# Token sum of phi(k) by eight accumulating DMAs instead of 32 matmuls, in a linear-attention and MLP-mixer kernel

## Chip, cores, metric

One core of one Trainium2 chip. The metric is the device time of one execution in microseconds (us), lower is better. The kernel before takes 267.94 us (median of 6 runs, 267.54 to 268.09, so 0.2% apart).

## The reference, cut to what matters

```python
B, S, D = 1, 2048, 640;  H = 32; Dh = 20
q, k, v = ...                                   # from x @ wqkv
phi = lambda t: jnp.where(t > 0, t + 1, jnp.exp(t)) + 1e-6
pq, pk = phi(q), phi(k)
kv  = jnp.einsum("bhsd,bhse->bhde", pk, v)
z   = jnp.einsum("bhsd->bhd", pk)               # the token sum: 640 numbers
den = jnp.einsum("bhqd,bhd->bhq", pq, z)[..., None] + 1e-6
o   = num / den                                 # then @ wo; this is branch a
# branch b: LayerNorm, W1, gelu, token shifts, W2, LayerNorm, W3, gelu, W4
return g * a + (1 - g) * b
```

The case is about `z`: the sum over 2048 tokens of `phi(k)`, and when the denominators that need it can be computed.

## The kernel before

TensorE (PE) runs as one long stream: the K stage (16 chunks of 128 tokens), the Q stage (10 units, with the x-times-phi(k) products "G" woven in), the W1 stage, W2, then W3 and W4. `pk` holds phi(k) as bf16, 128 partitions by 16 chunks by 640. The token sum is 32 narrow matmuls against ones, each onto 32 of the 128 output partitions, in turn onto the four groups of 32 (all 32 took 1.20 us in the trace), in the middle of the Q stage; two units later, ten one-column matmuls turn it into per-partition columns.

```python
def z_rows():                                   # after Q unit 2, counted from 0
    p = alloc()
    for (n0, n1) in COLS:                       # 512 + 128 columns
        for cc in range(0, NCH, 4):
            for q in range(4):
                mm(PP[p][32*q:32*(q+1), n0:n1], lhsT=ones32[:], rhs=pk[:, cc+q, n0:n1],
                   start=(cc == 0), stop=(cc == NCH-4), tile_position=(0, 32*q), ...)
    act(zsb[:], PP[p][:, 0:D], ACT.Copy)
    release(p)
    nc.vector.tensor_copy(zhi[:], zsb[:])       # high and low bf16 parts
    nc.vector.tensor_tensor(zlo[:], zsb[:], zhi[:], op=ALU.subtract)

def z_cols():                                   # after Q unit 4
    p = alloc()
    ...
    for j in range(DC):
        mm(PP[p][:, j:j+1], lhsT=zh[:, j], rhs=c32[:], start=True, stop=False)
        mm(PP[p][:, j:j+1], lhsT=zl[:, j], rhs=c32[:], start=False, stop=True)
    nc.vector.tensor_copy(zT[:], PP[p][:, 0:DC])
    release(p)
    for j in range(DC):                         # Zb: masks times column, for the denominators
        nc.vector.tensor_scalar(Zb[:, j, :], mask32, zT[:, j:j+1], None, op0=ALU.mult)
```

Two other users of POOL (GpSimd) matter, by their place in its program: in the trace, POOL stood 27.03 us at the copies that come first here, and the LayerNorm scales behind them started after them, at 33.24 us:

```python
# in late_loads(), before the K stage: waits for the load of W1
for g in range(4):
    nc.gpsimd.tensor_copy(w1x4[:, :, g, :], w1g[:, :, g, P:CG])

def ln1_sq(c):                                  # LayerNorm scale of four chunks at a time
    act(junk[:], x_sb[:, c, :], ACT.Square, accum_out=sq[:, c:c+1])
    if c % 4 == 3:
        ...                                     # five small POOL instructions -> rs1
def ln1_apply(c):                               # VectorE (DVE) needs rs1, then SP transposes by DMA
    nc.vector.tensor_scalar(lx[:], x_sb[:, c, :], me[:, c:c+1], rs1[:, c:c+1], ...)
    sp.dma_start_transpose(lnxT[:, :, c*P:(c+1)*P], lx[:])
```

And the start of the W1 stage:

```python
w1_unit(0, 4); den_unit(); rec_piece(0); w1_unit(0, 0); kv_unit(); rec_piece(1); w1_unit(0, 1)
m_unit(0); m_unit(1); ...
```

## Time and profile before

| | before |
|---|---|
| median time | 267.94 us |
| span of the profiled execution | 266.3 us |
| PE busy | 259.6 us (97%) |
| the 32 matmuls of the token sum, in the chain of waits | 1.20 us |

From the page of the kernel before: busy us per engine, then three rows over 40 equal slices of the span (6.66 us each) with the busy share of PE, the granted PE clock and the mean share of the 16 DMA engines, in tenths.

```profile
PE 259.6 (97%) x1666; PEld 136.1 (51%) x1699; DVE 116.0 (44%) x212; ACT 110.7 (42%) x165; POOL 32.9 (12%) x111
...
PE   7999999999999999999999999999999999999995
...
PEclk9999999999999999999999999999999999999999
DMA  6999993431340269932652001001000000001001
```

PE is never idle for long (97% busy) and never slow (mean granted clock 0.999), so the time is the length of its stream. The DMA row: from the second to the sixth slice (7 to 40 us) the DMA engines are full (9 in the row; a share of 1.04 to 1.32 in the windows from 13 to 40 us), because first x and then the weights for the later stages load then.

From the chain of work that ended last, in order of time (start, us, what): the token sum sits in it.

```profile
43.06 1.20 PE pp L364 x32
```

From the POOL timeline (start, us, instruction; in brackets the idle time before it and what ended it):

```profile
31.98 1.27 POOL L304 COPY w1x<-RB 128x160 bf16<-128x160 bf16 x4 [27.03 <-DMA RB<-in_B_w_dram]
33.24 0.23 POOL L218 TENSOR_SCALAR me<-ym 128x4 f32<-128x4 f32 x1
```

POOL stands for 27 us at the four copies that wait for the W1 load. Whatever is put behind them in POOL's program starts at about 33.3 us in this trace, and not before.

From the PE timeline, the first W1 unit, the denominators, and the second W1 unit:

```profile
73.59 2.32 PE L423 MATMUL pp<-lnxT,w1x 128*128 128x512 bf16 x10
75.84 1.26 PE L470 MATMUL pp<-pqT,Zb 128*32 128x512 bf16 x20
77.04 2.33 PE L423 MATMUL pp<-lnxT,RB 128*128 128x512 bf16 x9
```

A W1 unit costs PE about 2.2 us from start to next start.

### The profile page before, as it was taken

What the parts mean: (1) busy time and instruction counts of PE and PEld (TensorE: products, weight loads), DVE (VectorE), ACT (ScalarE), POOL (GpSimd) and SP (SyncE); (2) the same over time, 40 slices, a digit from 0 to 9 for tenths busy, and PEclk for the clock granted to TensorE, in tenths of its full rate; (3) what the DMA queues carried; (4) which work ended last, traced back from release to release, by engine and by line L of the source; (5) the groups of instructions that cost most, each with busy time, mean ns of one, the idle gap of its engine ahead of it and who ended that gap; (6) DMA issues with size and microseconds to landing.
All of it is one profiled execution on the core that took longest, in us unless ns stands there. A gap on an engine that the chain in (4) does not pass through costs nothing.

```text
span 266.3 us, 4195 instructions
## 1 busy us (share of the span) xinstructions
PE 259.6 (97%) x1666; PEld 136.1 (51%) x1699; DVE 116.0 (44%) x212; ACT 110.7 (42%) x165; POOL 32.9 (12%) x111
## 2 busy tenths in 40 slices
PE   7999999999999999999999999999999999999995
PEld 3555555555545445554444455555544444555552
DVE  2486748665655065999930033233200002233232
ACT  3466663665355771244977522022034444022020
POOL 5000132020200000536870000000000000000000
PEclk9999999999999999999999999999999999999999
DMA  6999993431340269932652001001000000001001
GB/s 204 169 192 301 365 225 68 62 75 25 77 98 0 59 213 362 313 83 49 101 100 49 0 2 49 27 25 49 27 25 0 2 0 0 25 27 49 27 25 49
DMA packets 42245, 23.95 MB, mean 90 GB/s; under 512 B 31090, under 2 KB 41458, under 8 KB 42226
## 3 DMA queue, kind: packets, MB, share of 16 engines
q1 hardware_dynamic: 41474, 22.99, 36.1%
q10 hardware_dynamic: 720, 0.69, 0.8%
q8 instruction: 13, 0.21, 0.3%
q14 instruction: 6, 0.05, 0.1%
q0 software_dynamic: 32, 0.00, 0.0%
HBM read 12.86 MB, written 3.44 MB: 61 GB/s over the span
## 4 chain that ended last, share of the span: by engine, by line
PE 95%; DMA 2%; issue 1%; DVE 0%; SPq 0%
PE pp L638 20%; PE pp L571 19%; PE pp L423 8%; PE pp L597 8%; PE pp L390 8%; PE pp L556 8%; PE pp L261 8%; PE pp L252 8%; DMA RXH<-in_A_x_dram 2%; PE pp L580 2%; PE pp L623 1%; PE pp L632 1%; PE pp L587 1%; PE pp L457 1%; PE pp L443 1%
## 5 line engine op out<-in xcount | busy, mean ns | idle before, releaser
L638 PE MATMUL pp<-RB,RXH 128*128 128x128 bf16 (+1 forms) x381 | 53.5, 297 | 0.7 <-issue 0.3
L571 PE MATMUL pp<-lnxT,RA 128*128 128x512 bf16 x235 | 51.9, 379 | 0.3
L638 PEld LDWEIGHTS <-RXH 128*128 128x128 bf16 x390 | 29.7, 98 | 24.2 <-issue 2.1
L571 PEld LDWEIGHTS <-RA 128*128 128x128 bf16 x240 | 23.4, 98 | 28.0
L600 ACT ACTIVATE RXH<-pp,g_all 128x640 f32<-128x640 f32 x16 | 12.7, 794 | 54.9 <-PE pp L597 54.9
L573 ACT ACTIVATE RXH<-pp 128x1024 bf16<-128x1024 f32 x24 | 24.2, 1019 | 26.7 <-PE pp L571 26.7
L244 ACT ACTIVATE eb<-pp 128x640 bf16<-128x640 f32 (+1 forms) x26 | 21.4, 828 | 25.2 <-PE pp L390 16.3
L261 PE MATMUL pp<-RPK,RXH 128*128 128x128 bf16 (+1 forms) x157 | 25.0, 297 | 0.2
L252 PE MATMUL pp<-RA,RXT 128*128 128x512 bf16 (+1 forms) x157 | 24.0, 300 | 0.2
L390 PE MATMUL pp<-RXT,RA 128*128 128x512 bf16 x97 | 23.1, 379 | 0.2
L597 PE MATMUL pp<-Mp,pqT 128*128 128x512 bf16 (+1 forms) x158 | 23.0, 298 | 0.1
L602 DVE SCALAR_TENSOR_TENSOR RPK<-RPK,omg,RXH 128x640 f32<-128x640 f32 x8 | 7.1, 885 | 36.5 <-ACT RXH L600 36.5
L556 PE MATMUL pp<-w,RXH 128*128 128x128 bf16 (+1 forms) x157 | 21.7, 297 | 0.2
L423 PE MATMUL pp<-lnxT,RB 128*128 128x512 bf16 x77 | 18.1, 379 | 0.2
L261 PEld LDWEIGHTS <-RXH 128*128 128x128 bf16 x160 | 12.7, 98 | 10.4
L247 DVE TENSOR_SCALAR eb<-eb 128x640 bf16<-128x640 bf16 (+1 forms) x26 | 9.5, 365 | 19.3 <-ACT eb L244 19.3
L602 DVE SCALAR_TENSOR_TENSOR RXT<-RXT,omg,RXH 128x640 f32<-128x640 f32 x8 | 7.1, 884 | 24.6 <-ACT RXH L600 24.6
L252 PEld LDWEIGHTS <-RXT 128*128 128x128 bf16 x160 | 12.6, 98 | 9.5 <-DVE RA L329 0.2
L597 PEld LDWEIGHTS <-pqT 128*128 128x128 bf16 x160 | 12.2, 98 | 10.0 <-issue 0.8
L556 PEld LDWEIGHTS <-RXH 128*128 128x128 bf16 x160 | 12.3, 98 | 9.6
L607 DVE SCALAR_TENSOR_TENSOR RXH<-pp,omg,RXT 128x640 bf16<-128x640 f32 x8 | 7.1, 884 | 19.8 <-PE pp L638 19.8
L390 PEld LDWEIGHTS <-RA 128*128 128x128 bf16 x100 | 11.1, 118 | 8.9
(110 smaller groups left out, 238.4 us busy)
## 6 DMA issues: line engine op xcount, KB each, us to landing
out_dram<-RXH SPq DMA_DIRECT2D x15, 160.0 KB, 1.8
RA<-in_B_w_dram SPq DMA_DIRECT2D x5, 432.0 KB, 6.9
RA<-in_A_wqkv_dram SPq DMA_DIRECT2D x2, 800.0 KB, 8.9
RB<-in_B_w_dram SPq DMA_DIRECT2D x1, 1120.0 KB
RXH<-in_A_x_dram SPq DMA_DIRECT2D x2, 480.0 KB, 4.7
RB<-in_B_w_dram SPq DMA_DIRECT2D x1, 960.0 KB, 13.6
RB<-in_B_w_dram SPq DMA_DIRECT2D x1, 800.0 KB, 8.5
Mp<-Mscr SPq DMA_DIRECT2D x1, 800.0 KB
```

The costliest lines, as they stand in the source:

```text
L244: act(e[:, 0:n], src, ACT.Exp)
L252: mm(PP[p][:, n0:n1], lhsT=xT[:, dc, c * P:(c + 1) * P], rhs=wkg[:, dc, n0:n1], start=(dc == 0), stop=(dc == DC - 1))
L261: mm(PP[p][:, n0:n1], lhsT=x_sb[:, c, i * P:(i + 1) * P], rhs=pk[:, c, n0:n1], start=(c == 0), stop=(c == NCH - 1))
L390: mm(PP[p][:, tt * 512:(tt + 1) * 512], lhsT=wqp[:, dc, j], rhs=xT[:, dc, t0:t0 + 512], start=(dc == 0), stop=(dc == DC - 1))
L423: mm(PP[p][:, tt * 512:(tt + 1) * 512], lhsT=lh, rhs=lnxT[:, dc, t0:t0 + 512], start=(dc == 0), stop=(dc == DC - 1))
L556: mm(PP[p][:, n0:n1], lhsT=hsT[:, fc, 2 + c * P:2 + (c + 1) * P], rhs=w2[:, fc, n0:n1], start=(fc == 0), stop=(fc == DC - 1))
L571: mm(PP[p][:, k * 512:(k + 1) * 512], lhsT=w3[:, dc, (fc + k) * P:(fc + k + 1) * P], rhs=lnxT[:, dc, t * 512:(t + 1) * 512], start=(dc == ...
L573: act(h2T[:, t % 2, fc:fc + 2, :], PP[p][:].rearrange("p (k s) -> p k s", k=2), ACT.Gelu_apprx_tanh)
L597: mm(PP[p][:, n0:n1], lhsT=pqT[:, j, c * P:(c + 1) * P], rhs=Mp[:, j, n0:n1], start=(j == 0), stop=(j == DC - 1))
L600: act(ga, PP[p][:, 0:D], ACT.Copy, scale=g_all[:, c:c + 1])
L602: nc.vector.scalar_tensor_tensor(x1(c), x1(c), omg[:, c:c + 1], ga, op0=ALU.mult, op1=ALU.add)
L638: mm(PP[p][:, n0:n1], lhsT=h2T[:, k, fc, cc], rhs=w4[:, fc, n0:n1], start=False, stop=(fc == NF - 1))
```

## The change

The intent: take the 1.2 us of matmuls off PE. The sum over chunks becomes eight DMAs of two chunks each (bf16 source, float32 destination, with `accum_op` add from the second on), issued by POOL between the middle of the K stage and the end of the Q stage. Below, each of these DMAs is a link of the chain, and the moment when its data have arrived is its landing. Each waits for the one before, as they update the same bytes. A DVE addition joins the two halves, and the column matmuls move from the Q stage behind the first W1 unit.

```diff
-    Mp = sb("Mp", DC * D)[:].rearrange("p (j d) -> p j d", j=DC)
+    RMP = sb("RMP", DC * D)
+    Mp = RMP[:].rearrange("p (j d) -> p j d", j=DC)
+    zacc = RMP[:, 0:4 * D].bitcast(F32)
 (ones32 and c32 become onec, one column of ones)
+    def z_add(k):
+        nc.gpsimd.dma_start(zacc, RPK[:, 2 * k * D:2 * (k + 1) * D],
+                            **({"accum_op": ALU.add} if k else {}))
+    def z_sum():
+        nc.vector.tensor_tensor(zsb[:], zacc[:, 0:D], zacc[:, D:2 * D], op=ALU.add)
+        nc.vector.tensor_copy(zhi[:], zsb[:])
+        nc.vector.tensor_tensor(zlo[:], zsb[:], zhi[:], op=ALU.subtract)
 (K stage, after chunk c)
+        if c in (9, 12, 15):
+            z_add(c // 3 - 3)
 (Q stage, after unit n_; z_rows is gone)
-            if n_ == 2:
-                z_rows()
-            if n_ == 4:
-                z_cols()
+            if n_ in (1, 3, 4, 6, 7):
+                z_add({1: 3, 3: 4, 4: 5, 6: 6, 7: 7}[n_])
 (end of the Q stage)
+    z_sum()
 (W1 stage)
     w1_unit(0, 4)
+    z_cols()
+    w1_unit(0, 0)
     den_unit()
     rec_piece(0)
-    w1_unit(0, 0)
     kv_unit()
```

More of the change, by code (lines that the diff above doesn't have):

```diff
@@ L103 @@
     ident = sb("ident", P)
-    ones32 = sb("ones32", 32)
-    c32 = sb("c32", 1)
+    onec = sb("onec", 1)
     mask4 = sb("mask4", P)
@@ L181 @@
         nc.gpsimd.memset(wkg[:, dc, D + 1:D + 2], 1.0)
-    nc.gpsimd.memset(ones32[:], 1.0)
-    nc.gpsimd.memset(c32[:], 1.0 / 32)
+    nc.gpsimd.memset(onec[:], 1.0)
     nc.gpsimd.memset(nhalf[:], -0.5)
@@ L342, with z_cols @@
         k_post(c, c)
+    def z_add(k):
[5 more added lines that the diff above has]
+        nc.vector.tensor_tensor(zlo[:], zsb[:], zhi[:], op=ALU.subtract)
+    def z_cols():
+        p = alloc()
+        zh = zhi[:].rearrange("p (q j) -> p j q", j=DC)
+        zl = zlo[:].rearrange("p (q j) -> p j q", j=DC)
+        for j in range(DC):
+            mm(PP[p][:, j:j + 1], lhsT=zh[:, j], rhs=onec[:], start=True, stop=False)
+            mm(PP[p][:, j:j + 1], lhsT=zl[:, j], rhs=onec[:], start=False, stop=True)
+        nc.vector.tensor_copy(zT[:], PP[p][:, 0:DC])
+        release(p)
+        for j in range(DC):
+            nc.vector.tensor_scalar(Zb[:, j, :], mask32, zT[:, j:j + 1], None, op0=ALU.mult)
     for c in range(3, NCH):
@@ L353 @@
             pop(ln1_s)
+        if c in (9, 12, 15):
+            z_add(c // 3 - 3)
     gq = [(0, c) for c in range(NCH - 3, NCH)] + [(i, c) for i in range(1, DC) for c in range(NCH)]
     wqp = wq.rearrange("p k (q j) -> p k j q", j=DC)
-    def z_rows():
-        p = alloc()
-        for (n0, n1) in COLS:
-            for cc in range(0, NCH, 4):
-                for q in range(4):
-                    mm(PP[p][32 * q:32 * (q + 1), n0:n1], lhsT=ones32[:], rhs=pk[:, cc + q, n0:n1],
-                       start=(cc == 0), stop=(cc == NCH - 4), tile_position=(0, 32 * q), skip_group_check=True)
-        act(zsb[:], PP[p][:, 0:D], ACT.Copy)
-        release(p)
-        nc.vector.tensor_copy(zhi[:], zsb[:])
-        nc.vector.tensor_tensor(zlo[:], zsb[:], zhi[:], op=ALU.subtract)
-    def z_cols():
-        p = alloc()
-        zh = zhi[:].rearrange("p (q j) -> p j q", j=DC)
-        zl = zlo[:].rearrange("p (q j) -> p j q", j=DC)
-        for j in range(DC):
-            mm(PP[p][:, j:j + 1], lhsT=zh[:, j], rhs=c32[:], start=True, stop=False)
-            mm(PP[p][:, j:j + 1], lhsT=zl[:, j], rhs=c32[:], start=False, stop=True)
-        nc.vector.tensor_copy(zT[:], PP[p][:, 0:DC])
-        release(p)
-        for j in range(DC):
-            nc.vector.tensor_scalar(Zb[:, j, :], mask32, zT[:, j:j + 1], None, op0=ALU.mult)
     n_ = 0
```

## The prediction

> **What bounds it now.** The page gives PE 259.6 of 266.3 us busy (97%) at full granted clock, and the chain of waits is 95% PE. Time is the PE stream's length plus its stalls; other engines matter only where PE waits for them.
>
> **Removed.** The groups by line show the column sum as 32 matmuls; in the chain they hold PE from 43.06 for 1.20 us, with a 0.3 us issue gap just before. So about 1.25 us (0.5%) leaves the critical path. The ACT copy of the sum (0.70 us) goes too; nothing critical waited for it. That is the whole possible gain: faster by over 2% is practically excluded.
>
> **Moved.** The ten one-column matmuls (PE about 0.65 us, 51.3 to 51.9) and their DVE copy and five masks (0.95 us) move from mid Q stage to just behind the first W1 unit. There they follow a new DVE sum (about 0.82), cast (0.49) and subtract (0.82): 2.2 us that PE now waits for directly.
>
> **Added.** Eight DMAs issued by POOL, each 128 rows of 1280 bf16 in, f32 out (655 KB written); seven also read the old 655 KB. Each waits for the one before: a serial chain. It is meant to start mid K stage (about 21 us), but in POOL's program order the first stands behind the w1x copies, which waited 27 us for the W1 load and ran from 31.98 to 33.25 (POOL timeline). So the chain starts at about 33.3, not 21.
>
> Duration of one link d: the only POOL-issued DMA in the trace, 1.2 KB, took 3.5 us to land, beside loads. [...] I take 5.4. The first competes with weight loads that land until about 42 (DMA share about 1.0 from 30 to 40): 6.3. No accumulating DMA is in the trace, so d is the weak number.
>
> Landing of the eighth (estimate): 33.3 + 6.3 + 7 x 5.4 = 77.4. DVE sum, cast, subtract: 79.6. PE, 1.25 + 0.65 us earlier than before, reaches the column matmuls at about 74.0. PE stall about 5.6 us, once, in the middle of the W1 stage; nothing later gives it back, since PE has no other slack. Had the chain been free, PE would still stand about 0.5 us at the denominators, because the masks queue on DVE behind the 1.7 us of shift copies.
>
> Sum: 267.9 - 1.25 + 5.6 = about **272.3 us** (+1.6%). Every 0.1 us of d is 0.7 us of the result; break-even near d = 4.8.
>
> Range, 8 in 10: 266.8 to 281. Chances: faster over 2% 0.01, within 2% 0.54, slower over 2% 0.45.
>
> **What would show it.** First new DMA issue at about 33.3 after the w1x copies; eight issues 5 to 6 us apart, the last landing at 74 to 81; the DVE sum of the two halves idle before it, released by that DMA; a PE idle of some us before the zhi weight loads at about 74; the K and Q stages unchanged except minus 1.9 us; every stage after shifted by one constant. LayerNorm scales of chunks 4 to 7 (POOL) come some us later, behind the third DMA; three free PSUM buffers should keep PE fed.
>
> **What would make it wrong.** d at or below 4.6: no stall, 266.7 to 267.5. [...] POOL, blocked in order, delaying LayerNorm scales enough that DVE holds up PSUM and PE stalls in the Q stage already. Transposes of the normalised rows slowed by the new traffic.

Where a cut is marked, the figures from which the author came to 5.4 us for a link, and one of the risks, have been taken out. The 5.4 us of a link and the 6.3 us of the first stand as guesses. The sum, with all its terms: 33.3 + 6.3 + 7 x 5.4 = 77.4 us for the eighth landing, from that a stall of 5.6 us, and 267.9 - 1.25 + 5.6 = 272.3 us.

## The result, and the profile after

The changed kernel takes 279.75 us (median of 6 runs, 278.53 to 281.56). Executions over 1.5% slower than the fastest of the same kernel are left out of the means. Ratios are computed as the mean time of one kernel's fast runs over that of the other's of the same rounds, so they are not quite the ratios of the medians; here 1.045, 95% interval 1.0406 to 1.0495. It is slower by 4.5%, where 1.6% was forecast.

The same lines of the page (a slice is now 7.0 us):

```profile
PE 261.1 (93%) x1635; PEld 135.8 (49%) x1667; DVE 116.3 (42%) x213; ACT 110.0 (39%) x164; POOL 40.2 (14%) x118
...
PE   8999999969905999999999999999999999999995
...
PEclk9999999999985999999999999999999999999999
DMA  6799999695896006995245200010010000001001
```

PE has a dent in the ninth slice, a hole in the twelfth, and in the thirteenth its clock is down as well. The rest is as before.

The POOL timeline after, reduced to the copies, the eight DMA issues, and one of the LayerNorm scale instructions (the last group ends likewise behind the eighth DMA):

```profile
34.05 1.11 POOL L304 COPY w1x<-RB 128x160 bf16<-128x160 bf16 x4 [29.14 <-DMA RB<-in_B_w_dram]
35.10 0.66 POOL L345 DMA_DIRECT2D RMP<-RPK  x1
...
46.05 0.96 POOL L345 DMA_DIRECT2D RMP<-RPK  x1 [8.03 <-DMA RMP<-RPK]
51.61 0.87 POOL L345 DMA_DIRECT2D RMP<-RPK  x1 [4.59 <-DMA RMP<-RPK]
...
53.67 1.05 POOL L222 TENSOR_TENSOR rs<-ve,nhalf 128x4 f32<-128x4 f32 x1
57.16 1.21 POOL L345 DMA_DIRECT2D RMP<-RPK  x1 [2.44 <-DMA RMP<-RPK]
63.65 0.87 POOL L345 DMA_DIRECT2D RMP<-RPK  x1 [5.29 <-DVE eb L247]
68.58 0.85 POOL L345 DMA_DIRECT2D RMP<-RPK  x1 [4.07 <-DMA RMP<-RPK]
...
73.51 1.11 POOL L345 DMA_DIRECT2D RMP<-RPK  x1 [1.83 <-DMA RMP<-RPK]
79.94 0.87 POOL L345 DMA_DIRECT2D RMP<-RPK  x1 [5.33 <-DMA RMP<-RPK]
```

The first link of the chain takes 10.95 us from issue to the next issue; the other six gaps are 5.56, 5.55, 6.49, 4.93, 4.93 and 6.43 us. (For one of the issues, at 63.65 us, the profile names a DVE instruction and not the landing as what ended POOL's wait; whether DVE's work delays an issue was not tested.) The time to landing of the eight, from the same DMAs' summary:

```profile
DMA to landing us min/median/max: 4.4/5.0/10.4
```

On DVE, the consequences (waits in brackets):

```profile
54.76 0.80 DVE L226 TENSOR_SCALAR lnxs<-RXH,me,rs 128x640 bf16<-128x640 bf16 x2 [6.99 <-POOL rs L222]
...
83.09 1.51 DVE L226 TENSOR_SCALAR lnxs<-RXH,me,rs 128x640 bf16<-128x640 bf16 x4 [6.54 <-POOL rs L222]
84.52 0.82 DVE L349 TENSOR_TENSOR zsb<-RMP 128x640 f32<-128x640 f32 x1
```

LayerNorm scales on POOL stand behind DMAs that wait; DVE waits for the scales, in order, and with it everything behind.

And on PE:

```profile
57.28 0.43 PE L261 MATMUL pp<-RPK,RXH 128*128 128x512 bf16 x2 [0.72 <-DVE pqT L248]
59.66 2.32 PE L390 MATMUL pp<-RXT,RA 128*128 128x512 bf16 x9 [1.95 <-DVE pqT L248]
...
74.55 2.32 PE L423 MATMUL pp<-lnxT,w1x 128*128 128x512 bf16 x10
85.92 0.20 PE L358 MATMUL pp<-onec,zhi 128*128 128x1 bf16 x1 [9.04 <-DVE zhi L350]
86.78 0.20 PE L359 MATMUL pp<-onec,zlo 128*128 128x1 bf16 x1 [0.66 <-DVE zlo L351]
...
87.97 3.62 PE L423 MATMUL pp<-lnxT,RB 128*128 128x512 bf16 x8 [0.22 <-issue]
91.52 1.27 PE L470 MATMUL pp<-pqT,Zb 128*32 128x512 bf16 x20
```

The W1 unit after the long wait runs from 87.16 to 91.52 us, 4.36 us in place of 2.17. The windows view of the same stretch shows why (window, its length, then busy us with instruction counts for PE, PEld, DVE, ACT and POOL; the last three columns are the granted clock, the DMA share and GB/s):

```profile
78.00:80.00 2.00, 0.00 (x0) 0.00 (x0) 0.00 (x0) 0.00 (x0) 0.06 (x1) 1.00 1.01 136
80.00:82.00 2.00, 0.00 (x0) 0.00 (x0) 0.00 (x0) 0.00 (x0) 1.68 (x5) 0.83 0.56 117
...
84.00:86.00 2.00, 0.08 (x1) 0.09 (x1) 1.93 (x5) 0.00 (x0) 0.00 (x0) 0.50 0.41 82
...
88.00:90.00 2.00, 2.00 (x5) 0.73 (x5) 1.85 (x9) 0.00 (x0) 0.00 (x0) 0.50 1.00 97
...
92.00:94.00 2.00, 2.00 (x39) 1.46 (x32) 1.12 (x2) 0.71 (x1) 0.00 (x0) 1.00 0.00 0
```

Some 4.5 us after PE went idle (76.9 us) its clock was halved (a mean of 0.83 from 80 to 82 us puts the step at 81.3), and it stayed halved until about 91.6. The two gaps in the Q stage (0.72 and 1.95 us, with two wide matmuls between them) left the clock full (1.00 in every window from 54 to 68 us).

The account of the 13.6 us between the two profiled spans: minus 1.25 us (matmuls and the gap ahead of them), plus 2.67 us (two gaps in the Q stage), plus 9.70 us (waits for zhi and zlo), plus 2.19 us (slow W1 unit) is 13.3 us.

### The profile page after: what moved, and what is told of

It reads as the page before. It is cut to its first block, busy times and chain, and to the rows that moved or that the text cites. A ratio compares the mean times of both kernels' runs of the same rounds, so it can differ in the third digit from the quotient of the medians.

```text
span 279.9 us, 4156 instructions
## 1 busy us (share of the span) xinstructions
PE 261.1 (93%) x1635; PEld 135.8 (49%) x1667; DVE 116.3 (42%) x213; ACT 110.0 (39%) x164; POOL 40.2 (14%) x118
## 4 chain that ended last, share of the span: by engine, by line
PE 69%; DMA 14%; SPq 7%; DVE 4%; POOL 2%; issue 2%; ACT 1%; POOLq 0%; DVEq 0%
PE pp L639 19%; PE pp L572 18%; DMA RMP<-RPK 11%; PE pp L598 8%; PE pp L557 8%; PE pp L423 8%; SPq L158 6%; DMA RB<-in_B_w_dram 3%; PE pp L581 2%; DVE lnxs L226 1%; PE pp L624 1%; SPq L155 1%; PE pp L633 1%; PE pp L308 1%; DVE pqT L248 1%
## 5 line engine op out<-in xcount | busy, mean ns | idle before, releaser
L639 PE MATMUL pp<-RB,RXH 128*128 128x512 bf16 (+1 forms) x382 | 53.9, 298 | 0.4
L574 ACT ACTIVATE RXH<-pp 128x1024 bf16<-128x1024 f32 x24 | 24.3, 1020 | 26.7 <-PE pp L572 26.7
L598 PE MATMUL pp<-RMP,pqT 128*128 128x128 bf16 (+1 forms) x156 | 22.8, 297 | 0.2
L423 PE MATMUL pp<-lnxT,RB 128*128 128x512 bf16 x78 | 19.9, 408 | 0.4 <-issue 0.4
L428 ACT ACTIVATE RXH<-pp 128x1024 bf16<-128x1024 f32 x8 | 8.2, 1027 | 22.0 <-PE pp L423 22.0
L390 PEld LDWEIGHTS <-RA 128*128 128x128 bf16 x100 | 11.2, 117 | 11.1 <-issue 2.0
```

What stands on the lines that cost most here:

```text
L390: mm(PP[p][:, tt * 512:(tt + 1) * 512], lhsT=wqp[:, dc, j], rhs=xT[:, dc, t0:t0 + 512], start=(dc == 0), stop=(dc == DC - 1))
L423: mm(PP[p][:, tt * 512:(tt + 1) * 512], lhsT=lh, rhs=lnxT[:, dc, t0:t0 + 512], start=(dc == 0), stop=(dc == DC - 1))
L574: act(h2T[:, t % 2, fc:fc + 2, :], PP[p][:].rearrange("p (k s) -> p k s", k=2), ACT.Gelu_apprx_tanh)
L598: mm(PP[p][:, n0:n1], lhsT=pqT[:, j, c * P:(c + 1) * P], rhs=Mp[:, j, n0:n1], start=(j == 0), stop=(j == DC - 1))
L639: mm(PP[p][:, n0:n1], lhsT=h2T[:, k, fc, cc], rhs=w4[:, fc, n0:n1], start=False, stop=(fc == NF - 1))
```

## The experiments

In all of them "before" ran on the same chip.

### e1: only the first DMA

```diff
-        if c in (9, 12, 15):
-            z_add(c // 3 - 3)
+        if c == 9:
+            z_add(0)
 (no z_add in the Q stage)
```

> Only the first of the eight DMAs is issued (wrong result on purpose: the token sum then holds four of sixteen chunks at most); the DVE sum, the cast, the column matmuls and the masks stay where the change put them. Theory A (the serial chain of eight DMAs is what costs): PE waits at the zhi weight loads fall from 9.7 us to under 0.7 us, both Q-stage PE gaps (2.7 us) are gone, time 266.7 to 267.6 us, so 1.2 us of removed matmuls minus about half a microsecond at the denominators. Rival B (the new place of sum, columns and masks costs by itself): 269 us or more. Neither expects the slow W1 unit after the gap (4.4 us against 2.2) to stay, if it comes from idle.

Measured: 267.1 us, ratio 0.9974 (0.9957 to 0.9992). Both Q-stage gaps and the wait for zhi are gone and the clock stays full; PE waits 0.79 us for the masks. The one DMA still took 10.7 us to land. So the new place of the sum and columns gives back some 0.4 of the 1.25 us (0.85 us lie between the medians), and all of the loss comes with the other seven links.

### e2: the LayerNorm scales ahead of the DMAs that block them

```diff
+        if c == 9: z_add(0)                    # K stage
+            for k in {1: (1, 2, 3), 5: (4, 5), 9: (6, 7)}.get(n_, ()):   # Q stage
+                z_add(k)
```

> Same eight DMAs, but POOL's LayerNorm scale groups stand before the DMAs that blocked them (one DMA, groups 0 and 1, three DMAs, group 2, two DMAs, group 3, two DMAs). Theory A (the landing of the eighth DMA sets the time, 84.4 us in the profile): the two Q-stage PE gaps (0.7 and 1.95 us) vanish, but PE then waits about 2.7 us longer for zhi, and the time stays at 279 to 280.5 us. Rival C (POOL blocked in order, which holds up DVE and so PE, is a cost of its own that adds): 277 us or less, the gap before zhi stays at 9 to 10 us.

Measured: 279.8 us, ratio 1.0448 (1.0416 to 1.048): no change. PE and then DVE of this kernel, at the columns:

```profile
84.29 0.20 PE L358 MATMUL pp<-onec,zhi 128*128 128x1 bf16 x1 [10.27 <-DVE zhi L350]
85.15 0.20 PE L359 MATMUL pp<-onec,zlo 128*128 128x1 bf16 x1 [0.66 <-DVE zlo L351]
```

```profile
82.88 0.83 DVE L349 TENSOR_TENSOR zsb<-RMP 128x640 f32<-128x640 f32 x1 [9.64 <-DMA RMP<-RPK]
```

The gaps in the Q stage have gone, PE arrives earlier, and waits longer for the same landing. The gaps in front of a fixed deadline cost nothing here. Rival C falls: POOL's blocking is visible in the trace of the changed kernel, and worth nothing by itself. Here the DVE sum is released by the eighth DMA directly, so this kernel is the base for most of what follows. Its chain runs from 33.64 to about 82.9 us.

### e3: the w1x copies out of the way

The four copies move on POOL from before the first DMA to behind the sixth.

> The w1x copies, which wait for the W1 load, move on POOL from before the first DMA to behind the sixth. Theory A with the copies as the gate: the first DMA issues at about 13 us, the second at about 24 us behind the first scale group; with links of 8 to 10 us while weights load and 5.5 us after, the eighth lands at 66 to 76 us and the time falls to 267 to 270 us. Rival D (the loads own the DMA engines until 42 us, whatever the issue time, so nothing is gained by issuing earlier): the eighth lands after 82 us, time 278 us or more.

Measured: 277.77 us, ratio 1.0376 (1.035 to 1.0402). The expectation missed. POOL and then PE of this kernel:

```profile
12.96 0.61 POOL L341 DMA_DIRECT2D RMP<-RPK  x1 [8.03 <-DVE eb L247]
...
31.11 1.05 POOL L222 TENSOR_TENSOR rs<-ve,nhalf 128x4 f32<-128x4 f32 x1
32.12 0.97 POOL L341 DMA_DIRECT2D RMP<-RPK  x1
43.14 0.87 POOL L341 DMA_DIRECT2D RMP<-RPK  x1 [10.05 <-DMA RMP<-RPK]
```

```profile
22.46 2.13 PE L252 MATMUL pp<-RA,RXT 128*128 128x512 bf16 x10 [3.68 <-DMA RXT<-in_A_x_dram]
```

The first DMA did issue at 13 us, but the second stands behind the first scale group, which waits for ACT, and issued at 32.1. What is more, in this run PE stood 3.68 us in the K stage for a load of x that had not arrived, and the second and third links took 11.0 and 10.5 us. The gate was real, but behind it is the same full set of DMA engines (9 in the page's DMA row from 14 to 62 us). The eighth landed at about 81.4 us (the DVE sum that it releases starts at 81.38), and most of the time stayed lost.

### e4: four W1 units ahead of the columns

```diff
     w1_unit(0, 4)
+    for fc in range(4):
+        w1_unit(0, fc)
     z_cols()
+    w1_unit(1, 4)
     den_unit()
 (key-value and M units between the second half's W1 units; scaling of the queries at the end)
```

> The chain is untouched; PE gets four more W1 units (8.9 us of useful work) before the column matmuls, and the later W1 units are woven with the key-value and M units instead. Theory A: the wait for zhi shrinks from 9.7 us to under 2 us, the slow clock after it goes, time 267 to 270 us (the 2.7 us in the Q stage stay: nearer 269.5). Rival E (the DMA traffic slows PE or the other engines throughout): still above 274 us.

Measured: 276.74, 277.03 and 279.68 us (a fourth run was slow), ratio 1.0373. The wait for zhi shrank as expected (the trace has 0.55 us, for zlo), but the time did not. PE of this kernel:

```profile
86.29 0.58 PE L423 MATMUL pp<-lnxT,w1x 128*128 128x512 bf16 x1 [2.55 <-DMA lnxT<-lnxs]
...
129.53 27.75 PE L567 MATMUL pp<-lnxT,RA 128*128 128x512 bf16 x118 [3.18 <-DMA lnxT<-lnxs]
```

Two new stalls, each followed by half clock (0.50 from 86 to 88 us; 0.66 on average from 130 to 135). The first: the second half's rows hang on the last LayerNorm scales, which here still stand behind the eighth DMA. The second comes from my order: five scalings of the queries (3.1 us of DVE) stand ahead of the W2 additions, and the loads of w3 and w4, issued later, meet the transposes of the second LayerNorm; e4 does not separate the two. So it says nothing for rival E; e5 repeats it without these faults.

### e5: everything that does not need the sum goes first

On top of e2: W1 units, key-value and M units before the columns, the DVE sum behind the key-value masks, the reciprocals after them, the scaling of the queries in the W3 stage.

```diff
     w1_unit(0, 4); w1_unit(0, 0); kv_unit(); w1_unit(0, 1); m_unit(0); m_unit(1)
     w1_unit(0, 2); m_unit(2); m_unit(3); w1_unit(0, 3); m_unit(4); m_unit(5)
+    z_sum(); m_move(); (loads of w3)
+    w1_unit(1, 4); z_cols(); w1_unit(1, 0); den_unit(); four rec_piece
     w1_unit(1, 1); w1_unit(1, 2); rexp_unit(); w1_unit(1, 3)
```

> Scale groups as in e2, chain untouched; everything that does not need the token sum (four W1 units, key-value and M units, 13.7 us of PE work after the first W1 unit) now stands before the column matmuls, the DVE sum behind the key-value masks, the denominators' reciprocals and the scaling of the queries later, where DVE was idle in the profile before. Theory A (chain's end near 83 us is the only thing that costs): no PE wait above 0.7 us for zhi or masks, no half clock, 266.4 to 267.4 us, faster than before by 0.2 to 0.6 per cent. Rival E (the links' traffic costs by itself[...]): 269 us or more.

Measured: 267.24 us against 267.78, ratio 0.9985 (0.9948 to 1.0023): the 12 us are back, but no gain is shown. The same chain still ended at 82.9 us, as DVE shows:

```profile
82.88 0.82 DVE L349 TENSOR_TENSOR zsb<-RMP 128x640 f32<-128x640 f32 x1 [4.16 <-DMA RMP<-RPK]
```

PE no longer asked before it. Rival E falls. PE waits 0.86 us for the masks. The kernel before was not run in this order, so what the order is worth by itself is not separated, here and in e11 and e12.

### e6: half of each row, and e7: no addition

Both on top of e2, each wrong. e6 moves 640 of 1280 elements per DMA (and doubles one half: its output still passed the comparison, so that passing proves little about this sum). e7 drops `accum_op`.

> As e2, but each DMA moves half of its row (640 of 1280 elements, wrong result on purpose). If bytes decide a link, the links behind the first fall from 5.6 us to about 3 us and the eighth lands by 65 us; if a fixed part decides, to 4 to 4.5 us[...], the eighth lands near 70 to 73 us and the time is 267 to 268.5 us.

> As e2, but the eight DMAs overwrite and do not add (wrong result on purpose): same issue, same waits, same bytes written, no read of the destination. If the read of the old sum costs, links behind the first fall by 0.8 to 1.5 us to 4.1 to 4.8 us and the eighth lands at 73 to 78 us, time 268 to 274 us; if it is free, the links stay at 5.4 to 5.7 us and the time at 279 to 280 us.

Measured: e6 274.73 us, e7 275.54 us. Both were gated late by my own order: the seventh DMA stands behind the last scale group, which waited for ACT until 67.8 and 68.2 us, and was issued at 69.3 and 69.8 us. So the times do not compare (both missed what was expected, with two runs each), but the landings do (min / median / max): e2 4.4 / 5.2 / 9.7, e6 3.3 / 3.8 / 9.0, e7 3.2 / 3.4 / 9.6 us. Adding to the old sum costs 1.8 us of a median link (5.2 against 3.4). Half the bytes save 1.4 us, so about 2.4 us of the 5.2 do not scale with bytes (3.8 minus 1.4; an estimate from these two medians). And the largest, the first link, is 9.0 us even with half the bytes, against 9.7 in e2: its length hardly depends on its own bytes.

### e8: PE kept busy while it waits

On top of e2, 42 dummy matmuls of 128x512 on the zero tile between the first W1 unit and the columns.

> As e2 with 42 dummy matmuls of 128x512 (about 9 us at full clock) on the zero tile between the first W1 unit and the column matmuls, so PE waits for the same landing but is not idle. If the half clock after the gap is caused by the idle PE, it disappears and the time falls by 2.0 to 2.6 us against e2, to 277.2 to 278 us; if the clock drop has another cause, the time stays at 279.8 us.

Measured: 277.44, 277.92 and 278.13 us (a fourth run was slow), against 279.0 to 280.6 of e2. The granted clock is 1.0 throughout, and the W1 unit after the wait takes 2.29 us, from its start to that of the denominators at 87.40:

```profile
85.11 2.32 PE L423 MATMUL pp<-lnxT,RB 128*128 128x512 bf16 x10
```

So the slow clock is the idle PE's, and costs about 2 us on top of the wait. (Between the two profiled runs lie 2.25 us, of which 0.42 are an earlier landing, 82.46 us in e8; e2 and e8 ran on different chips.)

### e9: the weight loads later

On top of e2, the loads of wv, wo and w2 are issued at the fifth Q unit (from 55.8 us in the trace).

> As e2, but the loads of the value, output and second MLP weights (wv, wo, w2, 2.4 MB), which shared the DMA engines with the first link until about 42 us, are issued about 10 us after that, at the fifth Q unit (about 50 us). If the first link's 10 us is contention with these loads, it falls to 4.5 to 6 us, and the links that then meet the loads (issued after 50 us) grow by some us in their place; the eighth lands at 78 to 83 us and the time stays within 275 to 280 us. If the first link is long for a reason of its own (first use of the queue), it stays at about 10 us.

Measured: 284.62 us, ratio 1.0636 (1.0615 to 1.0657), slower than expected. The windows view at the first link, which was issued at 33.37 us (last two columns: DMA share and GB/s):

```profile
34.00:35.00 1.00, 1.00 (x11) 0.53 (x8) 0.12 (x1) 1.00 (x2) 0.72 (x4) 1.00 0.61 225
35.00:36.00 1.00, 1.00 (x8) 0.59 (x7) 0.90 (x2) 1.00 (x3) 0.92 (x2) 1.00 1.18 425
36.00:37.00 1.00, 1.00 (x7) 0.51 (x6) 0.64 (x1) 0.16 (x1) 0.92 (x3) 1.00 0.08 13
```

Alone on the DMA engines (share 0.00 from 32 to 34 us and from 37 to 41), the first link was done after about 3.2 us (the smallest landing of this kernel), not 10. The second waited for its scale group until 41.0, so the gain was not used; and the fifth, which met the moved loads, took 12.0 us to the next issue (59.53 to 71.52). The cost goes with the loads: the link that met them was done about when they were (the large load of w2, issued at 58.70 us, took 11.8 us to land).

### e10: two accumulators, two chains of four

The second accumulator lies where the K weights were; the DMAs alternate.

```diff
+    zaccs = [RMP[:, 0:4 * D].bitcast(F32), RA[:, 0:4 * D].bitcast(F32)]
+        nc.gpsimd.dma_start(zaccs[k % 2], RPK[...], **({"accum_op": ALU.add} if k > 1 else {}))
+        for h in range(2):                      # in z_sum
+            nc.vector.tensor_tensor(zsb[:], zsb[:], zaccs[1][:, h*D:(h+1)*D], op=ALU.add)
```

> As e2, but two accumulators and so two chains of four links, interleaved on POOL: the same DMAs and bytes (one accumulating DMA fewer), a wait for every second DMA only, two more DVE additions (1.6 us). If the waiting for completions[...] is what the chain pays, three pairs of about 8 us after the first pair (13 to 15 us) end at 71 to 74 us, PE waits 2 to 5 us for zhi, 271 to 274 us. If the DMA engines' throughput limits, the end stays near 83 us and the time at 280 us or more.

Measured: 270.68 us (268.94 to 271.98), ratio 1.0103 (1.0063 to 1.0142), slightly better than expected. The same bytes written, but the last two were issued at 59.7 and 63.2 us in the trace, with median landings of 7.1 and 7.9 us in the two chains, so the end is at about 71 us (estimate from these) in place of 82.9. So a second chain takes some 12 of the single chain's 49 us away (up to 1.8 of them, by e7, because one link fewer adds to an old sum). e10 also issues its DMAs at earlier places in POOL's program, but in e2 POOL had always been idle for 2.3 us or more before it issued a link behind the first, so its places did not hold that chain up. PE still waits 1.95 and 0.66 us for zhi and zlo; DVE began the sum at 73.4 us, held by its last LayerNorm rows, which waited for transposes. And these short waits were followed by a lower clock too (7 in the page's PEclk row for the slice from 74.3 to 81.0 us); the W1 unit behind the columns took 3.94 us, to 81.67, in place of 2.17. At half clock for the first 3.5 us and full clock after, it would take as long (an estimate from these two times):

```profile
77.73 4.00 PE L425 MATMUL pp<-lnxT,RB 128*128 128x512 bf16 x10
```

The four runs fall apart by their clock: 271.73 and 271.98 us at 0.992 and 0.994, 268.94 and 269.63 us at 1.0 and 0.998.

### e11: e5 with the masks earlier

The columns move one W1 unit forward, so that the masks stand on DVE ahead of the second shift copies.

> As e5, with the column matmuls one W1 unit earlier, so that the masks stand on DVE before the second half's shift copies, and the denominators one unit earlier. The 0.9 us PE wait for the masks seen in e5 disappears; time 266.2 to 267 us, 0.3 us below e5 and 0.4 to 0.6 per cent below before, if nothing else waits.

Measured: 267.32 us (266.18 to 269.58), ratio 0.9997 (0.9962 to 1.0032). The wait for the masks is gone, as expected; now PE waits 0.47 us for zlo in the profiled run, since the chain ended at about 84.4 us this time. No gain is shown, where 0.4 to 0.6 per cent were expected.

### e12: two chains and the deferred order

> The two accumulators of e10 with the deferred order of e11: the chains end near 70 us, some 15 us before PE asks for the sum, so their scatter can no longer reach PE. If the deferral's remaining scatter (e11: 266.2 to 269.6 us) came from the chain's end lying close to PE's need, the runs lie at 266.2 to 267.2 us, 0.3 to 0.6 per cent below before, with an interval that excludes equality. If the traffic itself disturbs (transposes of the rows waiting behind it), they stay at 267 to 269 us with the same scatter.

Measured: 266.61 us (265.99 to 267.50) against 267.98, ratio 0.9951 (0.9921 to 0.9982): faster than both kernels, by 0.5%. PE runs into the columns without a wait:

```profile
84.97 0.81 PE L456 MATMUL pp<-RB,kvT 120*120 120x512 bf16 x4
85.72 0.20 PE L360 MATMUL pp<-onec,zhi 128*128 128x1 bf16 x1
```

DVE had zlo ready at 82.3 us. The intent of the change is now met: 1.37 us between the medians, against 1.25 us of PE work removed. That the two agree so well is not shown to be more than luck, as the new order was not run without the change.

## Why the prediction was wrong, point by point

- **What bounds the kernel, and what is removed: right.** With the chain made harmless the kernel came out at 266.6 to 267.3 us (e1, e5, e11, e12), against 267.8 to 268.0 for the kernel before; the interval excludes equality in e1 and e12 only.
- **The mechanism: right.** A serial chain behind the w1x copies ends after PE asks for the sum; PE waits for it in front of the columns, and no later stage gives it back. e1, e2 and e5 show it. The forecast stall was 5.6 us; 9.70 us were measured, and 10.93 us in e2.
- **The step that failed: "Landing of the eighth (estimate): 33.3 + 6.3 + 7 x 5.4 = 77.4".** It landed at about 82.9 us in e2, and at about 84.3 in the changed kernel (79.94 plus the 4.4 us of an undisturbed landing). Of this sum the term 6.3 was mis-sized: "The first competes with weight loads that land until about 42 (DMA share about 1.0 from 30 to 40): 6.3." The first link took 10.29 us in e2 and 10.95 in the changed kernel, plus 4.0 and 4.65. The numbers for it stood in the sentence: beside these loads the first link ended about when their backlog did, at 42 us or later (in e2 the DMA share is 1.09 to 1.16 from 33 to 42 us and 0.89 from 42 to 44, and the second link was issued at 43.93; e6: 9.0 us with half the bytes; e9: 3.2 us without the loads). The start was 0.3 us late in e2 and 1.8 us late in the changed kernel's profile; over these traces the copies start anywhere from 31.8 to 34.1 us. The seven others took 5.56 us each in e2 (43.93 to 82.88 us), as against 5.4.
- **A term that was left out: the clock.** "PE stall about 5.6 us, once" had no cost after the stall. The long wait was followed by half clock, which cost 2.19 us in the profile and about 2 us by e8. Such a wait need not be long: in other traces a lower clock also followed stalls of 3.68 us (e3: 7 in the PEclk row for the slice from 20.7 to 27.6 us), 3.18 and 2.55 us (e4: 0.66 from 130 to 135 us, 0.50 from 86 to 88), and 1.95 and 0.66 us with a one-column matmul between them (e10). After the 2.55 us of e4 the clock fell 2.1 us after PE's last matmul (a wait of 0.55 us and ten one-column matmuls stood just before it; 0.96 on average from 84 to 86 us puts the step at 85.8). In the changed kernel the clock fell 4.5 us after PE went idle and was full again about 4.4 us after steady matmuls resumed.
- Together: 272.3 plus 5.5 us of later landing (e2) plus about 2.2 us of slow clock is 280.0; 279.75 was measured. (In the profiled run of the changed kernel the landing was 6.9 us late: 281.4 by the same sum, 281.56 measured.)
- **"three free PSUM buffers should keep PE fed": wrong**, by 2.67 us of gaps in the Q stage of the changed kernel, listed among what could make the prediction wrong. But it moved nothing in the total (e2), as PE only waited less later.
- **The estimate of a link's size.** I took 5.4 us, a guess that no trace of that time showed. For 128 rows of 1280, bf16 to float32, the runs show 4.4 us to landing at the least (e2), and medians of 4.8 (e4) to 5.5 us (e3) in the kernels with one chain of full links; without the addition 3.4 us median (e7), and 3.2 us for e9's first, which adds to nothing. That the other 1 us of a typical link is traffic, such as row transposes, was not tested.

Open: why the first link takes 9.0 (e6) to 11.1 us (e11) to land beside the weight loads, and 3.2 us without them (e9); the runs show only the landings. Also open is why the W1 load's arrival varies by 2 us between runs (the copies behind it start from 31.84 us in e4 to 34.05 in the changed kernel).

## What to carry to other kernels

Work moved from the busiest engine to a serial chain of DMAs cost nothing here only where the first use came behind the chain's end or within half a microsecond of it (e5, e11, e12). That end has to be counted with the slowest moment of the DMA queues (here the first link, 10.95 us against 4.93 to 6.49 for the others); find that end first, and reorder the consumer before shortening the chain. A stall in front of a fixed deadline was free here (e2); a PE stall can be dearer than it looks, because a lower clock can follow it, here after stalls of 2.6 us in all (e10: a W1 unit of 3.94 us in place of 2.17) and more. Independent accumulators shortened the chain with the same bytes written (here 4.5% slower became 1.0% slower, and 0.5% faster together with the reordering).
